# Sixteen copies of the bias table in DRAM, and tail products from the main bias tiles

## The chip, the cores and the metric

The kernel runs on one core of one Trainium2 chip. A time is device microseconds of one execution. TensorE is called PE here, VectorE DVE, ScalarE ACT, GpSimd POOL and SyncE SP, as in the profile. The core has 16 DMA engines, which serve all its queues: SP and ACT issue hardware DMAs (queues q1 and q10 of the profile), POOL issues software DMAs (q0), which can also convert from float32 to bfloat16 on the way.

## What is computed

Attention with a relative position bias for 8 batches, 8 heads, 576 positions and 64 dimensions each, and behind it a bilinear feed-forward layer:

```python
scores = scale * np.matmul(q, k.transpose(0, 1, 3, 2))      # scale = 1/8
bias = bias_table[bucket]                                   # bucket: of |i - j|, 32 buckets, table 32 x 8
scores = scores + bias.transpose(2, 0, 1)[None, :, :, :]
attn = softmax(scores)                                      # over the last axis
x = (attn @ v), heads side by side                          # 4608 x 512
out = ((x @ w_a) * (x @ w_b)) @ w_out                       # w_a, w_b: 512 x 1536, w_out: 1536 x 512
```

All inputs and the output are float32. Distances of 128 and more have one bucket, the last. The softmax does not change if that bucket's bias is taken from every score, so a product with exp(bias - last bias) is needed only near the diagonal.

## The kernel before

**Tiling.** Heads are worked in 32 pairs: pair p is batch p // 4 and heads 2 (p % 4) and the next. The 576 positions are 4 tiles of 128 (the main part) and a tail of 64. For a pair, `qk1(p, t)` computes the transposed scores of key tile t against 512 queries for both heads, `ex(p, t)` (L346, ACT) takes exp, `mul(p, t)` (L354, DVE) multiplies the blocks near the diagonal with the bias tile `W_sb[p % 4]`. `qk_tail` and `ex_tail` (L373, L374) do the same for scores with tail keys or tail queries, into `att_sb`. `mul_tail(p)` (L380, L383) multiplies the tail's blocks near the diagonal: columns 896 to 1088 of `att` (tail keys against the last query tile and the tail queries), and a block of the last key tile against the tail queries. In these columns the partitions 0 to 63 belong to the first head of the pair and 64 to 127 to the second. `av` (L396, L405) multiplies with v, whose extra column of ones gives the sum, and `norm` (L413, L414) divides.

**The bias.** bt_sb is the table less its last row (L207, DVE), eb_sb its exp (L218, ACT). A product with a one-hot matrix (L220, PE) gives exp(bias) by distance, 256 entries for each head, copied into tab_sb between ones (L223, DVE) and written to a DRAM tensor `bias_tab` of 8 x 512 bfloat16 (L224, SP). From it the bias tiles are read back with a shift of one element per partition: `W_sb[hp]` (L167), 128 partitions x 2 heads x 384 elements, so 256 packets of 768 B; and `Wt_sb` (L228), a table for the tail, 64 partitions x 4 pairs x 192 elements for each of two heads, so 512 packets of 384 B in two DMAs. All partitions of one W read from the same two rows of 1 KB.

**The start.** For batch 0, q and k of pairs 0 to 2 come as float32 over SP and ACT (L130, `load32`), with their tails (L146, `load_pad`), and are transposed on PE (L511, L552). `warm_up` (L214) is matmuls on zeros. POOL clears buffers until 9.35 us, and then issues, in this order: v of batch 0, its tail, q and k of pair 3, w_a and w_b in parts (L159), q and k of batch 1, v of batch 1, more of w_a and w_b, q and k of batch 2 and their tails, w_out as one DMA (L164, tile `wo`), v of batch 2 and so on. `gate(2)` and `gate(3)` hold the loads of W2 and W3 on SP until DVE has come to a point of pairs 0 and 1.

**The order of the work.** It is written out by hand: the code's order is each engine's order (`manual_schedule`). The first four pairs run in a loop of their own, L561 and following lines; from pair 4 on each step weaves units of the feed-forward layer (`ff_a` L460 and L464, `ff_b` L470 and L473, `ff_o` L480 and L484) between the parts of attention. The units run in the order of 512-row chunks, so the first `ff_o` of chunk 0 comes in the step of pair 8; it is the first to need `wo`. From pair 8 on q and k are transposed by DMA instead of PE (`turn`, L322 and L327, SP), and the attention output of most pairs also (`t_x`, L429 and L432, SP). Every DMA carries one of 8 semaphores of its kind (8 for hardware DMAs, 8 for software DMAs), in turn, and is issued only when the eighth before it has landed.

Of the kernel before, what the change touches and what calls it, by code (L numbers as in the profile page):

```python
# [13 lines left out]
def kernel(  # L14
# [11 lines left out]
    nc = tc.nc  # L26
    FP32 = mybir.dt.float32
    BF16 = mybir.dt.bfloat16
    ACTF = mybir.ActivationFunctionType
    MULT = mybir.AluOpType.mult  # L30

    B, H, S, Dh = 8, 8, 576, 64
    NB = 32
# [12 lines left out]
    const = ctx.enter_context(tc.tile_pool(name="const", bufs=1))  # L46
    wpool = ctx.enter_context(tc.tile_pool(name="wpool", bufs=1))
# [13 lines left out]

    NR = 256
    TB = 512
    n_arr = np.abs(np.arange(NR) - NR // 2)
    half = NB // 2
    is_small = n_arr < half
# [12 lines left out]
    cst = const.tile([128, 128 + NR], BF16, name="cst_sb")  # L79
    ident = cst[:, 0:128]  # L80
    bt_sb = const.tile([128, H], FP32, name="bt_sb")
    bl_sb = const.tile([128, H], FP32, name="bl_sb")
    eb_sb = const.tile([128, H], BF16, name="eb_sb")
    tab_sb = const.tile([128, TB], BF16, name="tab_sb")
    zero_sb = const.tile([128, 512], BF16, name="zero_sb")
    tab = nc.dram_tensor("bias_tab", [H, TB], BF16, kind="Internal")
    W_sb = [wpool.tile([128, 2, 384], BF16, name=f"W{hp}") for hp in range(H // 2)]
    Wt_sb = wpool.tile([128, H // 2, 192], BF16, name="Wt")
    att_sb = [wpool.tile([128, 1152], BF16, name=f"att{i}") for i in range(2)]
    id32 = const.tile([128, 128], FP32, name="id32")  # L90
    q32 = const.tile([128, 3, NM, 2, Dh], FP32, name="q32")
# [2 lines left out]
    kt32 = const.tile([128, H // 2, 2, Dh], FP32, name="kt32")  # L94
# [49 lines left out]
    def load_pad(eng, src, dst, b, nb):  # L144
        for hh in range(2):
            eng.dma_start(  # L146
                out=dst[64 * hh:64 * hh + 64, 4 * (b % 2):4 * (b % 2) + 4 * nb, hh, 0:Dh],
                in_=src[b:b + nb, hh:H:2, SM:S, :].rearrange("b h c d -> c (b h) d"))
# [15 lines left out]
        nc.gpsimd.dma_start(out=wo_sb[:, :, :], in_=moe_w_out.rearrange("(t p) n -> p t n", p=128))  # L164

    def load_w(eng, hp):
        eng.dma_start(out=W_sb[hp][:, :, :],  # L167
                      in_=bass.AP(tensor=tab, offset=2 * hp * TB, ap=[[1, 128], [TB, 2], [1, 384]]))

    nc.sync.dma_start(out=bt_sb[0:NB, :], in_=bias_table)  # L170
    nc.scalar.dma_start(out=cst[:, :], in_=cst_handle.ap())
# [1 line left out]
                        in_=bass.AP(tensor=bias_table.tensor, offset=(NB - 1) * H,  # L173
                                    ap=[[0, NB], [1, H]]))
    def pad(eng, x, n):
        eng.memset(x[0:64, :, 1, 0:n], 0.0)
        eng.memset(x[64:128, :, 0, 0:n], 0.0)
# [5 lines left out]
    def load32(p, src, out, engs):  # L183
        for h in range(2):
            load_h(engs[h], src, out[:, p, :, h, :], 0, 2 * p + h)
# [6 lines left out]
    nc.vector.memset(zero_sb[:, :], 0.0)  # L192
    pad(nc.vector, kt32, Dh)
    pad(nc.vector, qt32, Dh)
    load_pad(nc.scalar, k, kt32, 0, 1)
    load_pad(nc.sync, q, qt32, 0, 1)
    nc.vector.memset(tab_sb[0:H, 0:127], 1.0)
    nc.vector.memset(tab_sb[0:H, 127 + NR:TB], 1.0)
    nc.vector.tensor_copy(out=id32[:, :], in_=ident)
    for i in range(2):  # L200
        nc.vector.memset(vm[i][:, :, :, Dh:Dh + 1], 1.0)
# [3 lines left out]
        for x in (ktl, qtl):  # L205
            pad(nc.gpsimd, x[i], Dh)
    nc.vector.tensor_tensor(out=bt_sb[0:NB, :], in0=bt_sb[0:NB, :], in1=bl_sb[0:NB, :],  # L207
                            op=mybir.AluOpType.subtract)
# [3 lines left out]
    def warm_up(n):  # L212
        for _ in range(n):
            nc.tensor.matmul(out=warm[:, :], lhsT=zero_sb[:, 0:128], rhs=zero_sb[:, :],  # L214
                             start=True, stop=True)

    warm_up(7)
    nc.scalar.activation(out=eb_sb[0:NB, :], in_=bt_sb[0:NB, :], func=ACTF.Exp)  # L218
    tps = ps_av.tile([128, 512], FP32, tag="av", name="tab_ps")
    nc.tensor.matmul(out=tps[0:H, 0:NR], lhsT=eb_sb[0:NB, :], rhs=cst[0:NB, 128:128 + NR],  # L220
                     start=True, stop=True)
    warm_up(2)
    nc.vector.tensor_copy(out=tab_sb[0:H, 127:127 + NR], in_=tps[0:H, 0:NR])  # L223
    nc.sync.dma_start(out=tab.ap(), in_=tab_sb[0:H, :])  # L224
    load32(2, q, q32, (nc.sync, nc.sync))
    load_w(nc.sync, 0)
    for hh in range(2):
        nc.sync.dma_start(out=Wt_sb[64 * hh:64 * hh + 64, :, :],  # L228
                          in_=bass.AP(tensor=tab, offset=hh * TB + 192,
                                      ap=[[1, 64], [2 * TB, H // 2], [1, 192]]))  # L230
    load32(2, k, k32, (nc.sync, nc.sync))
    load_w(nc.sync, 1)

    load_v(0)
# [142 lines left out]
    def mul_tail(p):  # L377
        hp = p % 4
        at, w = att_sb[p % 2], W_sb[hp]
        nc.vector.tensor_tensor(out=at[:, 896:1088], in0=at[:, 896:1088],  # L380
                                in1=Wt_sb[:, hp, ::-1], op=MULT)
        x = at[:, 0:512].rearrange("p (h t c) -> p h t c", h=2, t=NM)[:, :, NM - 1, :]
        nc.vector.tensor_tensor(out=x, in0=x, in1=w[:, :, 127:63:-1], op=MULT)  # L383

# [172 lines left out]
    def gate(hp):  # L557
        nc.vector.memset(W_sb[hp][0:1, 0, 0:1], 0.0)
        load_w(nc.sync, hp)

    for s in range(4):  # L561
        ex(s, 0)
        if s > 0:
            mul(s - 1, 3)
            mul_tail(s - 1)
# [58 lines left out]
    for s in range(4, NP + 1):  # L624
# [37 lines left out]
        for x in steps:  # L662
            if x is U:
                seen += 1
                n = (quota * seen + nu - 1) // nu - put
# [45 lines left out]
```

The softmax here doesn't subtract the row's maximum and nothing guards it: scores larger than these inputs give would overflow.

## Time and profile before

| | us |
|---|---|
| median of 5 runs | 445.08 |
| lowest, highest | 443.13, 447.65 |
| profiled execution | 446.2 |
| its span | 444.4 |
| PE busy | 414.8 (93%) |
| ACT busy | 242.5 (55%) |
| DVE busy | 192.8 (43%) |
| POOL busy | 115.1 (26%) |
| DMA queue q0 (POOL), share of 16 engines | 66.8% |
| DMA queue q1 (SP), share of 16 engines | 33.6% |

The profile is of one execution. A busy engine is one with an instruction in flight. A group's row names the line, the engine, the operation, output <- inputs, shapes and count, then total busy time and the mean time of one in ns, then the idle time of that engine just before such instructions and what ended it. A row of the timeline has start, duration, engine, line and operation, and in brackets the idle time before it and its releaser; SPq is the issuing of a DMA on SP. In a table by stretch, each engine has its busy time and number of instructions (PE, weight loads, DVE, ACT, POOL), and then come the granted PE clock, the mean number of packets in flight on a DMA engine (DMA share, which can exceed 1), and GB/s. The trace also records each DMA packet with queue, size and duration.

### The profile page before, as it was taken

What the parts mean: (1) busy time and instruction counts of PE and PEld (TensorE: products, weight loads), DVE (VectorE), ACT (ScalarE), POOL (GpSimd) and SP (SyncE); (2) the same over time, 40 slices, a digit from 0 to 9 for tenths busy, and PEclk for the clock granted to TensorE, in tenths of its full rate; (3) what the DMA queues carried; (4) which work ended last, traced back from release to release, by engine and by line L of the source; (5) the groups of instructions that cost most, each with busy time, mean ns of one, the idle gap of its engine ahead of it and who ended that gap; (6) DMA issues with size and microseconds to landing.
All of it is one profiled execution on the core that took longest, in us unless ns stands there. A gap on an engine that the chain in (4) does not pass through costs nothing.

```text
span 444.4 us, 8320 instructions
## 1 busy us (share of the span) xinstructions
PE 414.8 (93%) x3326; PEld 204.2 (46%) x3326; DVE 192.8 (43%) x468; ACT 242.5 (55%) x344; POOL 115.1 (26%) x152
## 2 busy tenths in 40 slices
PE   7396899599999999999999999999999999999995
PEld 3164344255444444444444444444444454444442
DVE  4265465324554355525552554355535550331320
ACT  4374766356665666666665666566656642322321
POOL 8678775057313600371026101100000000000000
PEclk9779999889999999999999999999999999999999
DMA  8999999999993997299819980941021002002004
GB/s 152 154 141 132 184 164 94 170 138 180 154 147 30 122 179 96 17 147 173 98 10 131 181 100 7 169 95 38 13 86 38 15 14 97 0 1 94 0 1 94
DMA packets 177191, 42.87 MB, mean 96 GB/s; under 512 B 163704, under 2 KB 172544, under 8 KB 177152
## 3 DMA queue, kind: packets, MB, share of 16 engines
q0 software_dynamic: 113232, 17.97, 66.8%
q1 hardware_dynamic: 62176, 23.88, 33.6%
q10 hardware_dynamic: 1744, 0.49, 0.6%
q8 instruction: 26, 0.43, 0.4%
q14 instruction: 13, 0.11, 0.1%
HBM read 38.83 MB, written 9.45 MB: 109 GB/s over the span
## 4 chain that ended last, share of the span: by engine, by line
PE 79%; DMA 15%; POOL 4%; issue 1%; ACT 0%; POOLq 0%
PE po L480 22%; PE pb L470 20%; PE pa L460 19%; PE av L405 7%; PE qk L335 6%; DMA wb<-in_moe_w_b_dram 6%; DMA wo<-in_moe_w_out_dram 5%; DMA vm<-in_v_dram 2%; DMA kn<-in_k_dram 2%; PE av L396 2%; PE qkt L360 1%; PE qkt L363 1%; POOL kn L124 1%; POOL vm L124 1%; PE qktt L366 0%
## 5 line engine op out<-in xcount | busy, mean ns | idle before, releaser
L346 ACT ACTIVATE at<-qk 128x1024 bf16<-128x1024 f32 x128 | 125.8, 1024 | 22.0 <-PE qk L335 22.0
L473 DVE TENSOR_TENSOR g<-pb,ha 128x512 bf16<-128x512 f32 x108 | 74.7, 692 | 127.4 <-PE pb L470 105.2
L460 PE MATMUL pa<-xn,wa 128*128 128x512 bf16 x432 | 111.1, 379 | 0.0
L470 PE MATMUL pb<-xn,wb 128*128 128x512 bf16 x432 | 110.9, 379 | 0.0
L480 PE MATMUL po<-wo,g 128*128 128x512 bf16 x432 | 104.4, 385 | 5.4 <-DMA wo<-in_moe_w_out_dram 5.4
L464 ACT ACTIVATE ha<-pa 128x512 f32<-128x512 f32 x108 | 64.6, 598 | 77.0 <-PE pa L460 77.0
L354 DVE TENSOR_TENSOR at<-at,W 128x512 bf16<-128x512 bf16 (+1 forms) x128 | 60.2, 484 | 13.6 <-ACT at L346 10.0
L480 PEld LDWEIGHTS <-g 128*128 128x128 bf16 x432 | 38.9, 99 | 53.2 <-issue 9.7
L470 PEld LDWEIGHTS <-wb 128*128 128x128 bf16 x432 | 38.7, 97 | 53.3 <-issue 18.0
L460 PEld LDWEIGHTS <-wa 128*128 128x128 bf16 x432 | 38.8, 98 | 49.6 <-issue 10.1
L484 ACT ACTIVATE ob<-po 128x512 f32<-128x512 f32 x36 | 21.5, 597 | 69.8 <-PE po L480 69.8
L124 POOL DMA_DIRECT2D vm<-in_v_dram x32 | 28.2, 895 | 102.2 <-PE av L405 98.7
L405 PE MATMUL av<-vm,at 128*128 128x65 bf16 x1024 | 48.0, 196 | 0.0
L405 PEld LDWEIGHTS <-at 128*128 128x128 bf16 x1024 | 43.3, 99 | 6.6
L413 DVE RECIPROCAL rc<-av 128x6 f32<-128x6 f32 x64 | 12.1, 189 | 59.6 <-PE av L405 59.6
L396 PE MATMUL av<-vt,att 128*128 128x130 bf16 x160 | 35.4, 221 | 0.4 <-DMA vt<-in_v_dram 0.4
L414 DVE TENSOR_TENSOR XG<-av,rc 128x384 bf16<-128x384 f32 x64 | 31.4, 491 | 4.2 <-DMA xn<-XG 2.1
L374 ACT ACTIVATE att<-qkt 128x1024 bf16<-128x1024 f32 x32 | 32.7, 1022 | 0.0
L124 POOL DMA_DIRECT2D qn<-in_q_dram x28 | 24.8, 906 | 25.5 <-DMA wo<-in_moe_w_out_dram 13.0
L335 PE MATMUL qk<-QTb,KTb 64*128 64x512 bf16 x192 | 29.1, 381 | 0.0
L124 POOL DMA_DIRECT2D kn<-in_k_dram x28 | 24.7, 892 | 14.1 <-DMA vt<-in_v_dram 6.6
L396 PEld LDWEIGHTS <-att 128*128 128x128 bf16 x160 | 15.9, 99 | 8.2 <-issue 0.9
(99 smaller groups left out, 204.8 us busy)
## 6 DMA issues: line engine op xcount, KB each, us to landing
out_dram<-ob SPq DMA_DIRECT2D x32, 256.0 KB, 3.7
vm<-in_v_dram POOLq DMA_DIRECT2D x32, 128.0 KB, 7.1
qn<-in_q_dram POOLq DMA_DIRECT2D x28, 128.0 KB, 10.8
kn<-in_k_dram POOLq DMA_DIRECT2D x28, 128.0 KB, 14.5
wa<-in_moe_w_a_dram POOLq DMA_DIRECT2D x6, 256.0 KB, 7.2
wb<-in_moe_w_b_dram POOLq DMA_DIRECT2D x6, 256.0 KB, 8.6
wo<-in_moe_w_out_dram POOLq DMA_DIRECT2D x1, 1536.0 KB, 22.3
out_dram<-ob SPq DMA_DIRECT2D x8, 128.0 KB, 2.3
```

Source lines behind the costliest of these rows:

```text
L124: nc.gpsimd.dma_start(out=(vm[b % 2][:, h0:h1, t, 0:Dh] if dst is None else dst[b % 2][:, :].rearrange("p (t h d) -> p t h d", h=H, t=NM)[ ...
L335: nc.tensor.matmul(out=ps[:, hh, :], lhsT=kT_(p, t)[r, :], rhs=qT[r, :, :], start=True, stop=True)
L346: nc.scalar.activation(out=at[:, :, :], in_=ps[:, :, :], func=ACTF.Exp, scale=scale)
L354: nc.vector.tensor_tensor(out=at[:, :, lo:hi], in0=at[:, :, lo:hi], in1=w[:, :, y:(None if z < 0 else z):-1], op=MULT)
L374: nc.scalar.activation(out=at[:, 0:1024].rearrange("p (a x) -> p a x", a=2), in_=ps[:, :, :], func=ACTF.Exp, scale=scale)
L396: nc.tensor.matmul(out=pav[:, slot, :, :], lhsT=x, rhs=vt[b // 2 % 2][:, 4 * i + hp, :, :], start=True, stop=True)
L405: nc.tensor.matmul(out=pav[:, slot, hh, :], lhsT=x, rhs=vm[i][:, 2 * hp + hh, t, :], start=False, stop=True, skip_group_check=True)
L460: nc.tensor.matmul(out=pa[:, :], lhsT=wa_sb[df // FW][:, mc, 128 * (df % FW):128 * (df % FW) + 128], rhs=xn_sb[mc][:, xin(c)], start=(mc = ...
L464: nc.scalar.activation(out=ha[:, :], in_=pa[:, :], func=ACTF.Copy)
L470: nc.tensor.matmul(out=pb[:, :], lhsT=wb_sb[df // FW][:, mc, 128 * (df % FW):128 * (df % FW) + 128], rhs=xn_sb[mc][:, xin(c)], start=(mc = ...
L473: nc.vector.tensor_tensor(out=g_sb[df][:, :], in0=pb[:, :], in1=ff["ha"][:, :], op=MULT)
L480: nc.tensor.matmul(out=po[:, :], lhsT=g_sb[df][:, 128 * tt:128 * tt + 128], rhs=wo_sb[:, df, :], start=(df == 0), stop=(df == NDF - 1))
```

## The change

- The DRAM table holds 16 copies of the 8 rows, 128 rows in all. To make them, exp is taken with a broadcast input into 16 x 8 columns of eb_sb, the one-hot product has 128 output rows, and the copy, the cleared borders and the write to DRAM have 128 rows.
- `load_w` becomes two DMAs, one for each head, of 128 packets of 768 B. Partitions 8r to 8r + 7 read from copy r.
- The tail table `Wt_sb` and its two DMAs are gone. `mul_tail` multiplies the 64 partitions of each head with the matching slice of `W_sb`, so it has three DVE instructions instead of two.
- On ACT, the load of the tails of k for batch 0 is issued behind exp instead of ahead of the bias memsets in the code's order.
- One warm-up matmul instead of two behind the one-hot product.

```diff
--- before.py
+++ after.py
@@ -61,6 +61,7 @@
 
     NR = 256
     TB = 512
+    NREP = 128 // H
     n_arr = np.abs(np.arange(NR) - NR // 2)
     half = NB // 2
     is_small = n_arr < half
@@ -80,12 +81,11 @@
     ident = cst[:, 0:128]
     bt_sb = const.tile([128, H], FP32, name="bt_sb")
     bl_sb = const.tile([128, H], FP32, name="bl_sb")
-    eb_sb = const.tile([128, H], BF16, name="eb_sb")
+    eb_sb = const.tile([128, NREP * H], BF16, name="eb_sb")
     tab_sb = const.tile([128, TB], BF16, name="tab_sb")
     zero_sb = const.tile([128, 512], BF16, name="zero_sb")
-    tab = nc.dram_tensor("bias_tab", [H, TB], BF16, kind="Internal")
+    tab = nc.dram_tensor("bias_tab", [NREP * H, TB], BF16, kind="Internal")
     W_sb = [wpool.tile([128, 2, 384], BF16, name=f"W{hp}") for hp in range(H // 2)]
-    Wt_sb = wpool.tile([128, H // 2, 192], BF16, name="Wt")
     att_sb = [wpool.tile([128, 1152], BF16, name=f"att{i}") for i in range(2)]
     id32 = const.tile([128, 128], FP32, name="id32")
     q32 = const.tile([128, 3, NM, 2, Dh], FP32, name="q32")
@@ -164,8 +164,11 @@
         nc.gpsimd.dma_start(out=wo_sb[:, :, :], in_=moe_w_out.rearrange("(t p) n -> p t n", p=128))
 
     def load_w(eng, hp):
-        eng.dma_start(out=W_sb[hp][:, :, :],
-                      in_=bass.AP(tensor=tab, offset=2 * hp * TB, ap=[[1, 128], [TB, 2], [1, 384]]))
+        for hh in range(2):
+            eng.dma_start(
+                out=W_sb[hp][:, hh, :],
+                in_=bass.AP(tensor=tab, offset=(2 * hp + hh) * TB,
+                            ap=[[H * TB + 128 // NREP, NREP], [1, 128 // NREP], [1, 384]]))
 
     nc.sync.dma_start(out=bt_sb[0:NB, :], in_=bias_table)
     nc.scalar.dma_start(out=cst[:, :], in_=cst_handle.ap())
@@ -192,10 +195,9 @@
     nc.vector.memset(zero_sb[:, :], 0.0)
     pad(nc.vector, kt32, Dh)
     pad(nc.vector, qt32, Dh)
-    load_pad(nc.scalar, k, kt32, 0, 1)
     load_pad(nc.sync, q, qt32, 0, 1)
-    nc.vector.memset(tab_sb[0:H, 0:127], 1.0)
-    nc.vector.memset(tab_sb[0:H, 127 + NR:TB], 1.0)
+    nc.vector.memset(tab_sb[:, 0:127], 1.0)
+    nc.vector.memset(tab_sb[:, 127 + NR:TB], 1.0)
     nc.vector.tensor_copy(out=id32[:, :], in_=ident)
     for i in range(2):
         nc.vector.memset(vm[i][:, :, :, Dh:Dh + 1], 1.0)
@@ -215,19 +217,17 @@
                              start=True, stop=True)
 
     warm_up(7)
-    nc.scalar.activation(out=eb_sb[0:NB, :], in_=bt_sb[0:NB, :], func=ACTF.Exp)
+    nc.scalar.activation(out=eb_sb[0:NB, :].rearrange("n (r h) -> n r h", h=H),
+                         in_=bt_sb[0:NB, :].unsqueeze(1).to_broadcast([NB, NREP, H]), func=ACTF.Exp)
+    load_pad(nc.scalar, k, kt32, 0, 1)
     tps = ps_av.tile([128, 512], FP32, tag="av", name="tab_ps")
-    nc.tensor.matmul(out=tps[0:H, 0:NR], lhsT=eb_sb[0:NB, :], rhs=cst[0:NB, 128:128 + NR],
+    nc.tensor.matmul(out=tps[:, 0:NR], lhsT=eb_sb[0:NB, :], rhs=cst[0:NB, 128:128 + NR],
                      start=True, stop=True)
-    warm_up(2)
-    nc.vector.tensor_copy(out=tab_sb[0:H, 127:127 + NR], in_=tps[0:H, 0:NR])
-    nc.sync.dma_start(out=tab.ap(), in_=tab_sb[0:H, :])
+    warm_up(1)
+    nc.vector.tensor_copy(out=tab_sb[:, 127:127 + NR], in_=tps[:, 0:NR])
+    nc.sync.dma_start(out=tab.ap(), in_=tab_sb[:, :])
     load32(2, q, q32, (nc.sync, nc.sync))
     load_w(nc.sync, 0)
-    for hh in range(2):
-        nc.sync.dma_start(out=Wt_sb[64 * hh:64 * hh + 64, :, :],
-                          in_=bass.AP(tensor=tab, offset=hh * TB + 192,
-                                      ap=[[1, 64], [2 * TB, H // 2], [1, 192]]))
     load32(2, k, k32, (nc.sync, nc.sync))
     load_w(nc.sync, 1)
 
@@ -377,8 +377,10 @@
     def mul_tail(p):
         hp = p % 4
         at, w = att_sb[p % 2], W_sb[hp]
-        nc.vector.tensor_tensor(out=at[:, 896:1088], in0=at[:, 896:1088],
-                                in1=Wt_sb[:, hp, ::-1], op=MULT)
+        for hh in range(2):
+            r, y = slice(64 * hh, 64 * hh + 64), 383 - 64 * hh
+            nc.vector.tensor_tensor(out=at[r, 896:1088], in0=at[r, 896:1088],
+                                    in1=w[r, hh, y:y - 192:-1], op=MULT)
         x = at[:, 0:512].rearrange("p (h t c) -> p h t c", h=2, t=NM)[:, :, NM - 1, :]
         nc.vector.tensor_tensor(out=x, in0=x, in1=w[:, :, 127:63:-1], op=MULT)
 
```

## The prediction

> **What bounds the kernel now.** I read the page first: span, engine shares, costliest groups.
>
> ```profile
> span 444.4 us, 8320 instructions
> ...
> PE 414.8 (93%) x3326; PEld 204.2 (46%) x3326; DVE 192.8 (43%) x468; ACT 242.5 (55%) x344; POOL 115.1 (26%) x152
> ...
> L480 PE MATMUL po<-wo,g 128*128 128x512 bf16 x432 | 104.4, 385 | 5.4 <-DMA wo<-in_moe_w_out_dram 5.4
> ```
>
> PE is idle for 444.4 − 414.8 = 29.6 us. A table of busy time by stretch shows where:
>
> ```profile
> 10.00:15.00 5.00, 3.12 (x23) 1.63 (x21) 1.40 (x3) 4.29 (x7) 5.00 (x8) 1.00 1.09 114
> 15.00:20.00 5.00, 0.00 (x0) 0.00 (x0) 2.70 (x8) 0.94 (x2) 2.12 (x3) 0.76 2.04 156
> ...
> 70.00:80.00 10.00, 9.31 (x80) 4.69 (x81) 5.73 (x15) 6.49 (x9) 3.52 (x5) 1.00 1.44 106
> 80.00:90.00 10.00, 4.57 (x36) 2.24 (x35) 3.05 (x8) 2.54 (x3) 0.88 (x1) 0.79 1.41 166
> 90.00:100.00 10.00, 10.00 (x86) 4.89 (x85) 3.11 (x9) 5.65 (x8) 5.24 (x6) 0.86 2.08 136
> 100.00:444.00 344.00, 339.52 (x2610) 162.73 (x2608) 145.33 (x337) 188.62 (x271) 53.84 (x65) 1.00 0.79 82
> ```
>
> The first number after the stretch is its length, the second PE's busy time; the last three are clock, DMA share, GB/s. From 100 to 444 PE lacks 4.48 us, all at the end, after its last matmul. So nothing there is worth time unless it stops PE, and the whole question is what happens before 88 us. Two waits stand there, in the timeline:
>
> ```profile
> 11.67 1.43 SPq L130 DMA_DIRECT2D k<-in_k_dram  x2
> 15.27 0.91 DVE L354 TENSOR_TENSOR at<-at,W 128x512 bf16<-128x512 bf16 x2 [3.65 <-DMA W<-bias_tab]
> 21.09 1.09 PE L511 MATMUL trk<-id,k 128*128 128x128 f32 x4 [6.54 <-DMA k<-in_k_dram]
> ...
> 65.39 1.02 POOL L164 DMA_DIRECT2D wo<-in_moe_w_out_dram  x1 [0.49 <-DMA kn<-in_k_dram]
> ...
> 87.75 1.89 PE L480 MATMUL po<-wo,g 128*128 128x512 bf16 x4 [5.43 <-DMA wo<-in_moe_w_out_dram]
> ```
>
> The second one decides. At 82.3 PE has nothing left that does not need wo and stands until 87.75. Whatever PE gains or loses before that, up to 5.43 us, disappears in this wait; only the landing of wo moves the end. Wo is late in POOL's queue, whose DMAs each wait for the eighth one before (this shows as waits for other loads):
>
> ```profile
> 16.18 0.75 POOL L130 DMA_DIRECT2D kn<-in_k_dram  x1 [0.55 <-DMA vm<-in_v_dram]
> 18.46 0.74 POOL L130 DMA_DIRECT2D kn<-in_k_dram  x1 [1.53 <-DMA vm<-in_v_dram]
> 20.32 0.74 POOL L159 DMA_DIRECT2D wa<-in_moe_w_a_dram  x1 [1.11 <-DMA vm<-in_v_dram]
> 23.00 0.74 POOL L159 DMA_DIRECT2D wb<-in_moe_w_b_dram  x1 [1.94 <-DMA vm<-in_v_dram]
> ```
>
> From 15.6 us on POOL issues as fast as its earlier loads land. So the change is worth what it gives to POOL's queue between its first load (9.35, first packets at 11.25) and about 30 us, when the bias tables have been read.
>
> **What the Trainium skill says.** (1) "DMA: Bandwidth & Descriptors", Queues, rings and completion order: each DMA engine takes turns between the queues that have work, packet by packet. The trace agrees: while W is read (12 to 13 us) POOL's queue moves 249 packets of 128 B, at 17 to 18 us, beside other loads of SP, 609. (2) The same page, Latency and other measured facts, has DMA rates halved by row pitches of 2 MiB and more and supposes aliased memory channels; on many engines reading one small table it says nothing. Here the same 768-B packets took 74 ns on average for W0, 51, 65 and 40 for W1 to W3, and 42 for the load of cst (128 different rows). (3) "VectorE: DVE Perf Modes", Two Vector instructions with no wait between them: an instruction that starts in another group of 32 partitions than the one before is held until that has finished. The trace has no such pair; it shows what is lost, L380 and L383 starting 0.17 us apart although L380 lasts 0.25. (4) "TensorE: Matmul & The Clock Gate", Part 1: an idle window of about 3.4 us halves the clock. The trace agrees: after the wait for wo it is 0.5 from 86.13 to 92.96, which costs PE half of 92.96 − 87.75, or 2.6 us.
>
> **The change, part by part, as time of POOL's queue.** The yardstick is the rate of all queues together where W isn't read: 863, 839 and 900 packets a us at 14, 15 and 17 us, so about 860.
>
> - Wt goes: 2 DMAs of 256 packets, 512 / 860 = 0.60 us, and 1.26 us of SP's issuing.
> - W0 from 16 copies: from 11.47 to 14.0 the engines moved 1,171 packets in 2.53 us, where 860 a us would be 2,176. The gap is 1,005 / 860 = 1.17 us. POOL's supply doesn't explain it (0.88 us for each 1,024 packets). But the copies only spread the reads over 16 places, 8,208 B apart, and each place still has 8 readers. Bounds 0 (no cure) and 1.2; I take 0.9.
> - W1 to W3: (11 + 25) ns × 256 above W3's 40 ns, over 16 engines, is 0.58 us; with a DMA share of some 1.6 (that many packets at once) it is 0.35. Bounds 0 and 0.6.
> - The order on SP. Hardware DMAs too wait for the eighth before them, and the moved kt load and the added W DMA shift these pairs: the k loads of pair 1 waited until 4.77 for a q load, and now wait for cst and the bias table, landed by 3.7. Exp waits only for the subtraction at 4.61 (0.36 us earlier, as the table load no longer stands behind the kt issues). Against it the table write grows from 8 to 128 packets, at 79 ns 8 on each engine instead of one, so 0.55 us more before W0. What of W0 is read before 11.25 meets no load of POOL. Bounds 0 and 1.0; I take 0.2.
>
> Sum 0.60 + 0.9 + 0.35 + 0.2 = 2.05 us; bounds 0.6 and 3.4.
>
> Costed at nothing:
> - The k load of pair 2 stands behind W0 alone instead of W0 and Wt. It should land near 17 instead of 21, PE restart, and then wait for vm and vt (23.5 now, earlier by about the sum). That is PE's gain, and it vanishes in the wait for wo. W's wait at 15.27 likewise.
> - The kt DMAs now stand on ACT behind exp, before the copy of QT (6.44): exp ends near 4.9, two issues take 1.35, so 6.25; they wait for a q and a k load that land near 5. They land 4.8 us after issue, near 10.4, for a transpose at 10.17. A slip of 1 us here reaches PE, but PE stands from 14.55 to 21.09 behind it. Four more SP issues of about 0.37 us for W, against two of Wt: SP waits for DVE's gates at 13 to 23 anyway.
> - The first W multiply waits for two DMAs instead of one; the second comes 0.4 us behind. Behind it on DVE is the copy of QT for pair 1 (18.91), which PE needs only after the k load.
> - Exp over 128 instead of 8 elements: at most the 0.38 us of the 256-wide copy instead of 0.21. The table product has 128 rows instead of 8 at the same 256 columns. One warm-up matmul (0.3 us) less, inside PE's wait for k and q.
> - The tail product: two of 0.25 us instead of one, held: 0.25 + 0.25 + 0.22 against 0.39 from L380's start to L383's end, +0.33 us, 32 times, 10.6 us of DVE (lower bound 0.17 each, if they overlap). Cover: I took every tail product from 100 to 366 us. The next DVE instruction starts at least 0.88 us after it, and the matmul that reads att at least 0.61 us after (once; else 1.25 or more). Without that cover it would be 28 × 0.33 = 9.2 us.
>
> The profiled execution took 446.2 us (span 444.4 and 1.8 around it), so 446.2 − 2.05 = 444.15. It lies 1.1 above the median of the runs, 445.08; against the median that is 443.0.
>
> **Rivals.**
> - The clock. If wo lands 2 us earlier and PE arrives at its wait no earlier, the wait is 3.4 us, and the half clock behind it (2.6 us) may be spared. 443.0 − 2.6 = 440.4. For: the wait would be as short as one window. Against: PE's start is freed too, and arrives earlier by about as much.
> - The reads are not cured: slow because of their odd byte offsets, or because 8 KB apart is the same place again. For: the offsets stay. Against: W3, with the same offsets, took 40 ns when it ran thinly. Only Wt's 0.6 us remains: 444.4.
> - Slower: the DMA transposes fall deeper into wo. Wo took 22.3 us because SP's transposes of qn, kn and XG run in it: 49 and 53 GB/s in 72 to 76 against 179 and 196 in 78 to 82. One us of that costs 1 − 51/185 = 0.72 us. They are issued in order, when PE, DVE and the qn and kn loads allow, and the change brings all of these forward by different amounts. From 2.05 / 0.72 = 2.8 us more overlap on, the kernel is slower than before. One more stretch of 4 us with the gain eaten gives 445.1 + 2.9 = 448.0; two, 450.9. Against: what they wait for are mostly POOL's own loads, which move with wo.
>
> **How the numbers follow.** Forecast 443.0 (441.7 to 444.2) has 0.50, the clock 0.18 (439 to 441.5), no cure 0.18 (444 to 445.5), slower 0.14 (446 to 451). The range 439.3 to 447.8 leaves out the ends of the clock case and the upper half of the slow case. A difference of 1% (4.45 us) is about what a measurement of this kernel can tell from no change. Faster by that, below 440.6: most of the clock case and the far tail of the forecast, 0.23. Slower, above 449.5: 0.09. Between: 0.68.
>
> **What would show it.** W's packets at 40 to 50 ns each; no wait for Wt; the k load of pair 2 landed near 17 us; POOL's kn, wa and wb issues 1 to 2 us earlier; the wait for wo ending near 85.7 instead of 87.75; DVE busy some 5 to 10 us more with PE still full from 100 us on. The prediction is wrong if wo's landing doesn't follow POOL's early issues (then the transposes decide), or if PE shows gaps behind tail products.

## The result, and the profile after

The changed kernel takes 444.23 us (median of 44 runs, 441.75 to 446.77); the kernel before, in runs beside it, 444.13 us (79 runs). The ratio is 1.0011, with a 95% interval of 0.9997 to 1.0024: no gain, and at most a quarter of a per cent of loss. Ratios here and below leave out executions that are over 1.5% above the fastest of their kernel and are estimated apart from the medians, which are of all executions, so they are not quite the quotients of these. The forecast was 443.0, range 439.3 to 447.8, with 0.68 for "within 1%". The range held, and so did "within 1%"; the 2.05 us of gain did not come, so the question is where they went.

The page of the changed kernel's profiled execution (445.21 us, of which 443.4 are its span), with the groups and the landing of `wo` that answer to those read before:

```profile
span 443.4 us, 8351 instructions
...
PE 415.0 (94%) x3325; PEld 204.7 (46%) x3325; DVE 203.4 (46%) x500; ACT 242.7 (55%) x344; POOL 115.1 (26%) x152
...
L482 PE MATMUL po<-wo,g 128*128 128x512 bf16 x432 | 103.2, 382 | 0.0
...
L335 PE MATMUL qk<-QTb,KTb 64*128 64x512 bf16 x192 | 29.5, 386 | 4.0 <-DMA KTb<-kn 4.0
...
L382 DVE TENSOR_TENSOR att<-att,W 64x192 bf16<-64x192 bf16 x64 | 15.9, 249 | 11.5 <-ACT att L374 11.0
...
wo<-in_moe_w_out_dram POOLq DMA_DIRECT2D x1, 1536.0 KB, 15.0
```

The wait of 5.4 us for `wo` is gone. In its place PE waits 4.0 us for `KTb`, the transposed k that SP's queue delivers. DVE has 10.6 us more work (203.4 against 192.8), nearly all of it in the tail product. Before, its first part was one instruction for each pair, 8.0 us in all (shortest, median and longest in ns):

```profile
L380 DVE TENSOR_TENSOR att<-att,Wt x32: 246/248/260, 18.6 to 360.7; 128x192 bf16<-128x192 bf16 x32
```

Now it is two, L382, 15.9 us in all; the rest of the 10.6 us is that the products of a tail no longer overlap. The table by stretch says where PE stands (length, then PE's busy time first; clock, DMA share and GB/s last):

```profile
10.00:15.00 5.00, 3.58 (x27) 2.07 (x26) 2.08 (x4) 4.57 (x7) 5.00 (x8) 1.00 0.96 91
15.00:20.00 5.00, 0.54 (x4) 0.10 (x2) 2.44 (x9) 1.93 (x3) 2.12 (x3) 0.92 1.87 167
...
70.00:80.00 10.00, 8.89 (x73) 4.33 (x72) 6.27 (x15) 5.84 (x10) 1.55 (x2) 1.00 1.35 168
80.00:90.00 10.00, 7.09 (x77) 3.86 (x74) 5.07 (x13) 5.29 (x8) 3.04 (x5) 1.00 1.97 132
90.00:100.00 10.00, 8.91 (x80) 4.61 (x81) 3.06 (x8) 4.85 (x7) 5.67 (x7) 0.83 1.99 163
100.00:444.00 344.00, 338.68 (x2605) 162.26 (x2603) 153.09 (x361) 187.85 (x269) 50.57 (x61) 1.00 0.76 79
```

From 100 us to the end of the span (343.4 us) PE lacks 4.7 us, much as the 4.48 us before (up to 444 us): the added DVE work costs nothing there. Everything is again decided before 92 us, in the timeline:

```profile
10.55 1.22 SPq L168 DMA_DIRECT2D W<-bias_tab  x2
11.81 1.14 SPq L130 DMA_DIRECT2D k<-in_k_dram  x2
...
17.51 0.91 DVE L354 TENSOR_TENSOR at<-at,W 128x512 bf16<-128x512 bf16 x2 [4.90 <-DMA W<-bias_tab]
18.50 0.75 POOL L130 DMA_DIRECT2D kn<-in_k_dram  x1 [2.13 <-DMA vm<-in_v_dram]
20.28 0.74 POOL L159 DMA_DIRECT2D wa<-in_moe_w_a_dram  x1 [1.03 <-DMA vm<-in_v_dram]
22.25 1.08 PE L513 MATMUL trk<-id,k 128*128 128x128 f32 x4 [6.71 <-DMA k<-in_k_dram]
22.61 0.74 POOL L159 DMA_DIRECT2D wb<-in_moe_w_b_dram  x1 [1.58 <-DMA vm<-in_v_dram]
...
63.40 1.02 POOL L164 DMA_DIRECT2D wo<-in_moe_w_out_dram  x1 [0.22 <-issue]
...
91.09 1.03 PE L335 MATMUL qk<-QTb,KTb 64*128 64x512 bf16 x4 [4.00 <-DMA KTb<-kn]
```

Almost nothing of the start has moved as forecast. The k of pair 2 is issued at 11.81 us, later than the 11.67 of before although the two loads of Wt between W0 and it are gone, and PE gets it at 22.25 instead of 21.09. The first product with W starts at 17.51 instead of 15.27. POOL's `kn`, `wa` and `wb` stand within 0.4 us of where they were (18.46, 20.32, 23.00). The issue of W0 takes 1.22 us (two DMAs) where one took 0.37 before:

```profile
9.95 0.37 SPq L167 DMA_DIRECT2D W<-bias_tab  x1
```

One caution: single executions of one kernel differ by 2 to 3 us in this stretch, as the runs below show. Times are therefore compared over many runs; a trace is only one execution, and counts for more where several kernels with the same edit agree.

### The profile page after: what moved, and what is told of

Same layout as the page of the kernel before. It is cut to its first block, busy times and chain, and to the rows that moved or that the text cites. A ratio compares the mean times of both kernels' runs of the same rounds, so it can differ in the third digit from the quotient of the medians.

```text
span 443.4 us, 8351 instructions
## 1 busy us (share of the span) xinstructions
PE 415.0 (94%) x3325; PEld 204.7 (46%) x3325; DVE 203.4 (46%) x500; ACT 242.7 (55%) x344; POOL 115.1 (26%) x152
## 4 chain that ended last, share of the span: by engine, by line
PE 85%; DMA 9%; DVE 2%; SPq 1%; ACT 1%; issue 1%; DVEq 0%; ACTq 0%
PE pb L472 22%; PE po L482 21%; PE pa L462 21%; PE av L407 8%; PE qk L335 7%; DMA KTb<-kn 3%; DMA k<-in_k_dram 2%; DMA xn<-XG 2%; PE av L398 2%; PE qkt L360 1%; PE qkt L363 1%; DMA q<-in_q_dram 1%; DMA bias_tab<-tab_sb 1%; ACT at L346 1%; DVE g L475 0%
## 5 line engine op out<-in xcount | busy, mean ns | idle before, releaser
L482 PE MATMUL po<-wo,g 128*128 128x512 bf16 x432 | 103.2, 382 | 0.0
L382 DVE TENSOR_TENSOR att<-att,W 64x192 bf16<-64x192 bf16 x64 | 15.9, 249 | 11.5 <-ACT att L374 11.0
```

The costliest lines, as they stand in the source:

```text
L482: nc.tensor.matmul(out=po[:, :], lhsT=g_sb[df][:, 128 * tt:128 * tt + 128], rhs=wo_sb[:, df, :], start=(df == 0), stop=(df == NDF - 1))
```

## The experiments

Times are medians, each ratio is against runs of the kernel before on the same chip. Where an expectation names a theory by a letter, the text around it says in words what is told apart.

### One part at a time

First: does the gain never arise, or does one part of the change give it and another take it? Four kernels, made from the kernel before. `p1_copies` has the 16 copies and the W loads in two DMAs, and keeps `Wt`:

```diff
+    NREP = 128 // H
...
+    tab = nc.dram_tensor("bias_tab", [NREP * H, TB], BF16, kind="Internal")
...
+        for hh in range(2):
+            eng.dma_start(
+                out=W_sb[hp][:, hh, :],
+                in_=bass.AP(tensor=tab, offset=(2 * hp + hh) * TB,
+                            ap=[[H * TB + 128 // NREP, NREP], [1, 128 // NREP], [1, 384]]))
```

> The kernel before with only the 16 copies and the W loads in two DMAs; tail table, order on ACT and warm-ups stay. Theory A (two chains of nearly equal length end at about 88 to 91 us: POOL's queue up to w_out, and table write, W0, k of pair 2, PE, XG, DMA transpose of k of batch 2; the larger table write makes the second longer): W0's multiply and the k of pair 2 come 0.5 to 1.5 us later than in before, ratio 1.001 to 1.004. Rival B (the start hardly matters, reads from copies cost the same as before): ratio 0.999 to 1.001, no shift. If the copies do cure the reads (the prediction): W packets at 40 to 50 ns, ratio 0.996 to 0.998.

Measured: 444.7 us, ratio 1.0013 [0.9993, 1.0033]. The copies alone give nothing; a loss of up to 0.3% is not excluded.

`p2_tail` has the tail product from W, and no `Wt`, with the table as before:

```diff
-    for hh in range(2):
-        nc.sync.dma_start(out=Wt_sb[64 * hh:64 * hh + 64, :, :], ...)
...
+        for hh in range(2):
+            r, y = slice(64 * hh, 64 * hh + 64), 383 - 64 * hh
+            nc.vector.tensor_tensor(out=at[r, 896:1088], in0=at[r, 896:1088],
+                                    in1=w[r, hh, y:y - 192:-1], op=MULT)
```

> The kernel before with only the tail product from the main W tiles (no tail table, three DVE instructions in a tail product); one table of 8 rows. Theory A: 512 packets less on both chains, k of pair 2 lands 1 to 2 us earlier, ratio 0.995 to 0.998. Rival B: ratio 0.999 to 1.001. A third reason, the longer tail product reaching PE: 1.005 or more, with gaps of PE behind tail products after 100 us.

Measured: 442.48 us, ratio 0.9943 [0.9921, 0.9966], so 2.5 us faster (1.5 to 3.5 by the interval; the medians differ by 1.95). Its timeline:

```profile
10.00 0.37 SPq L166 DMA_DIRECT2D W<-bias_tab  x1
10.41 1.03 SPq L129 DMA_DIRECT2D k<-in_k_dram  x2
14.69 0.91 DVE L349 TENSOR_TENSOR at<-at,W 128x512 bf16<-128x512 bf16 x2 [1.90 <-DMA W<-bias_tab]
17.64 1.09 PE L508 MATMUL trk<-id,k 128*128 128x128 f32 x4 [1.91 <-DMA k<-in_k_dram]
...
21.63 0.27 PE L393 MATMUL av<-vt,att 128*128 128x130 bf16 x1 [1.74 <-DMA vt<-in_v_dram]
...
86.05 1.89 PE L477 MATMUL po<-wo,g 128*128 128x512 bf16 x4 [5.57 <-DMA wo<-in_moe_w_out_dram]
```

With Wt out of the way k is issued 1.3 us earlier than before, PE has it 3.4 us earlier (17.64 against 21.09), and the first product with v starts at 21.63 instead of 23.70. The wait for `wo` is as long as before, but ends 1.7 us earlier (86.05 against 87.75).

`p3_order` moves the kt loads on ACT behind exp and drops the warm-up matmul:

```diff
-    load_pad(nc.scalar, k, kt32, 0, 1)
...
     nc.scalar.activation(out=eb_sb[0:NB, :], in_=bt_sb[0:NB, :], func=ACTF.Exp)
+    load_pad(nc.scalar, k, kt32, 0, 1)
...
-    warm_up(2)
+    warm_up(1)
```

> The kernel before with only the load of the tails of k moved behind exp on ACT and one warm-up matmul less. Theory A: the copy of QT on ACT and the first scores come up to 1 us later, but the table is written earlier; ratio 0.999 to 1.002. Rival B: 0.999 to 1.001. Were the later tails of k what eats the gain: 1.003 or more, with PE waiting for kt.

Measured: 444.89 us, ratio 0.9993 [0.9973, 1.0014]: harmless and useless. Its single trace has `wo` issued at 62.53 instead of 65.39 us, with no gain in the runs: an earlier issue of `wo` in one trace, as in the changed kernel's, is no proof of one.

`p0_notable` takes the bias tables away, to see what all their traffic costs. The table is neither written nor read, and every bias weight is one:

```diff
-    nc.sync.dma_start(out=tab.ap(), in_=tab_sb[0:H, :])
...
-    load_w(nc.sync, 0)
-    for hh in range(2):
-        nc.sync.dma_start(out=Wt_sb[64 * hh:64 * hh + 64, :, :], ...)
...
+    nc.vector.memset(W_one[:, :, :], 1.0)
```

> The kernel before with no bias table in DRAM at all: the write and all reads of W and Wt are left out, and the products near the diagonal are with ones, so the bias is left out of the scores. The most that any cheaper reading of the table could give. Theory A: the k of pair 2 lands near 13 instead of 21 us, then PE waits for v of batch 0 at about 21 to 22; both chains get about 2 us shorter; ratio 0.993 to 0.996. Rival B (the start hardly matters): 0.998 to 1.001. If the prediction's yardstick for the reads is right (all reads together cost POOL's queue some 3 us): 0.992 to 0.995 and the issue of w_out 3 us earlier.

Measured: 438.17 us, ratio 0.9851 [0.9818, 0.9883]. The bias traffic and SP's order around it cost 6.6 us, more than any of its expectations allowed. The k of pair 2 is there without a wait, and the first product with v starts 5.5 us earlier than before:

```profile
15.90 0.66 PE L501 MATMUL trk<-id,k 128*128 128x128 f32 x4
...
18.17 0.22 PE L386 MATMUL av<-vt,att 128*128 128x130 bf16 x1 [0.92 <-DMA vt<-in_v_dram]
```

The three parts alone multiply to 1.0013 × 0.9943 × 0.9993 = 0.9949; the whole has 1.0011, further off than their intervals together allow. They interact.

### Which part takes the gain

The tail part was put together with each of the other two. `p12_copies_tail` is the changed kernel without the edits of `p3_order`:

```diff
+    tab = nc.dram_tensor("bias_tab", [NREP * H, TB], BF16, kind="Internal")
...
-    Wt_sb = wpool.tile([128, H // 2, 192], BF16, name="Wt")
```

> The kernel before with the copies and with the tail product from W, but the old order on ACT and two warm-up matmuls. The tail part alone gave 0.9943, because the k of pair 2 landed at 17.6 instead of 21.1 us. Theory C: the copies take this back, since W0 in two DMAs is issued in 1.2 instead of 0.4 us, starts later and is no faster: k of pair 2 at 20 to 22.5 us, ratio 0.998 to 1.002. Rival D (the order on ACT takes it back): k of pair 2 at 17 to 18.5, ratio 0.993 to 0.996.

Measured: 444.67 us, ratio 1.0002 [0.9987, 1.0017].

`p23_tail_order` is the changed kernel without the copies:

```diff
-    load_pad(nc.scalar, k, kt32, 0, 1)
...
+    load_pad(nc.scalar, k, kt32, 0, 1)
...
-    Wt_sb = wpool.tile([128, H // 2, 192], BF16, name="Wt")
```

> The kernel before with the tail product from W and the new order on ACT, without the copies. Theory C: k of pair 2 at 17 to 18.5 us, ratio 0.993 to 0.996. Rival D: k of pair 2 at 20 to 22.5, ratio 0.998 to 1.002.

Measured: 442.52 us, ratio 0.9947 [0.9928, 0.9967]. So the moved loads on ACT leave the gain of the tail part alone, and the copies, which cost nothing clear by themselves, take all of it. Why they cost less beside `Wt` was not found. In the timeline of the kernel with copies and tail part:

```profile
9.93 1.21 SPq L168 DMA_DIRECT2D W<-bias_tab  x2
11.18 1.14 SPq L130 DMA_DIRECT2D k<-in_k_dram  x2
16.39 0.91 DVE L354 TENSOR_TENSOR at<-at,W 128x512 bf16<-128x512 bf16 x2 [3.59 <-DMA W<-bias_tab]
19.87 1.08 PE L513 MATMUL trk<-id,k 128*128 128x128 f32 x4 [4.14 <-DMA k<-in_k_dram]
```

W0 is asked for at the same time as in `p2_tail` (9.93 and 10.00), but it is issued for 1.21 us instead of 0.37, DVE has it 1.7 us later, and k 2.2 us later. These two executions took 444.34 us (`p2_tail`) and 441.97 (`p12_copies_tail`), the other way round from the medians: they show where the start differs, not that the difference in time comes from there. The records of W0's packets (768 B each, 256 of them; times from the timeline's zero) over the kernels that read it in this place, `d_pe_a` and `d_pool_a` of below included:

| kernel | copies | first packet after issue, us | first packet to last end, us | mean ns of a packet |
|---|---|---|---|---|
| before | no | 1.3 | 3.3 | 74 |
| p2_tail | no | 1.3 | 3.0 | 74 |
| p23_tail_order | no | 1.0 | 3.0 | 60 |
| p3_order | no | 1.4 | 2.4 | 50 |
| after | yes | 2.2 | 4.3 | 63 |
| p12_copies_tail | yes | 2.0 | 4.0 | 86 |
| p1_copies | yes | 1.9 | 3.2 | 69 |
| d_pe_a | yes | 1.8 | 3.7 | 72 |
| d_pool_a | yes | 1.4 | 2.6 | 65 |

With copies the packets are no faster, and in four of the five kernels they start 0.4 to 1.1 us later after the issue than without. The fifth, `d_pool_a`, starts as early as `p3_order`: there POOL's first packets move only at 15.3 us instead of 11.0. So it seems to take both for the late start, the longer issue and POOL's loads, which set in just as W0's packets are due; `d_pool_a` is a single trace.

### Is it the shared rows, and do 16 copies cure them?

`m_styles` reads 128 rows of 768 B from the table in a quiet stretch (375 to 432 us), two reads of each pattern one after the other, in three rounds:

```diff
+    styles = {"hot": [[1, 128], [1, 384]], "hot0": [[0, 128], [1, 384]],
+              "cop": [[H * TB + 8, 16], [1, 8], [1, 384]],
+              "own": [[TB + 1, 128], [1, 384]], "own0": [[TB, 128], [1, 384]]}
```

> The changed kernel, and near its end, where the DMA engines do little, 30 reads of 128 rows of 768 B from the table, pairs of reads one after the other, in five patterns three times: all partitions from one row with a shift of an element each (as before); all from one row without a shift; 16 copies as in the change; each partition its own row with a shift; each its own row without one. Only the packets count, not the time of the kernel. If many readers of one row are what is slow: the first two 70 ns, the others 36 to 45. If the odd start is: with a shift 49 or more, without 36, copies or not. If neither, and only other traffic makes them slow: all near 40.

Measured (one execution, whose total time says nothing here). The first read of each pattern overlaps the last of the pattern before it, so the table has the second reads, three of each, from the packet records and SP's issues:

| pattern | mean ns of a packet | first packet to last end, us | issue to last end, us |
|---|---|---|---|
| one row for all, shifted by an element per partition (W of before) | 61 to 71 | 1.62 to 1.67 | 2.6 to 2.75 |
| one row for all, not shifted | 39 to 54 | 1.50 to 1.59 | 2.45 to 2.55 |
| 16 copies, 8 shifted readers each (W of the changed kernel) | 52 to 60 | 1.19 to 1.21 | 2.5 |
| a row for each partition, shifted | 41 to 50 | 0.52 to 0.60 | 1.5 to 1.55 |
| a row for each partition, not shifted | 36 to 49 | 0.56 to 0.84 | 1.5 to 1.8 |

The landings over all reads (KB, median us from issue to landing):

```profile
scr_hot<-bias_tab SPq DMA_DIRECT2D x12, 96.0 KB, 3.5
scr_own<-bias_tab SPq DMA_DIRECT2D x12, 96.0 KB, 1.9
...
scr_cop<-bias_tab SPq DMA_DIRECT2D x6, 96.0 KB, 3.6
```

The names `hot` and `own` cover both forms, with and without shift. The odd start is not what is slow: a row of its own with the shift is as quick as without. A read in which many readers share one place is slow: 1.6 us against 0.55. With 8 readers in each of 16 places the packets are through in 1.2 us, so the copies spare 0.4 of the 1.1 us that rows of their own would. And most of that is given back in the issue: SP takes 0.52 us for the second read of the copies, 0.32 for the second reads of the other patterns, and the first packet follows 1.3 instead of 1.0 us after the issue. From issue to end the copies are nearly as slow as the single row, 2.5 against 2.6 to 2.75 us.

The single packet is not what grows. Its median is 34 to 44 ns in every pattern; what differs is how many are under way at once, on average 3 to 4 for the unshifted single row, 5 for the shifted one, 6 for the copies, 7 to 11 for rows of their own. The expectation, which looked at the time of a packet, does not decide here. Whether DRAM or the handing out of the packets to the engines holds them back was not tested.

### Is it the order on SP?

If the copies do harm because k of pair 2 stands behind a W0 that takes longer, putting k ahead of W0 must give the gain back. `a1_k_first` does that to the changed kernel, and `v1_k_first` to `p2_tail`:

```diff
     load32(2, q, q32, (nc.sync, nc.sync))
-    load_w(nc.sync, 0)
     load32(2, k, k32, (nc.sync, nc.sync))
+    load_w(nc.sync, 0)
     load_w(nc.sync, 1)
```

> The tail part alone, and the two loads of the k of pair 2 issued ahead of W0 on SP, in the time in which SP waits for the table write. Theory C (SP's chain over this k decides what PE has done when the transposes and w_out come): k lands by 15 us, PE next waits for v of batch 0 at 20 to 22 us, ratio 0.989 to 0.993. Rival E (only POOL's queue up to w_out sets the end): no better than the tail part alone, 0.993 to 0.996.

> The changed kernel with only the two loads of the k of pair 2 issued ahead of W0 on SP. Theory C (the copies take the gain of the tail part back because this k waits behind W0 and its longer issue): k lands by 16 us, the gain is back, ratio to before 0.992 to 0.996. Rival F (what the copies cost is the later W0 itself, and with it the first products on DVE): W0 even later, ratio 0.998 to 1.002.

Measured: `v1_k_first` 441.49 us, 0.9928 [0.9904, 0.9952]; `a1_k_first` 442.53 us, 0.9968 [0.9949, 0.9988]. The first interval holds values of both its theories. The second ratio is just above what its theory C expected (0.992 to 0.996); against the changed kernel's 1.0011 it is 0.43%, or 1.9 us, better. First the timeline of `v1_k_first`, then that of `a1_k_first`:

```profile
9.11 1.05 SPq L129 DMA_DIRECT2D k<-in_k_dram  x2
14.42 0.91 DVE L349 TENSOR_TENSOR at<-at,W 128x512 bf16<-128x512 bf16 x2 [1.83 <-DMA W<-bias_tab]
15.45 0.66 PE L508 MATMUL trk<-id,k 128*128 128x128 f32 x4
```

```profile
8.70 0.92 SPq L130 DMA_DIRECT2D k<-in_k_dram  x2
10.41 11.34 SPq L168 DMA_DIRECT2D W<-bias_tab  x8
15.46 0.66 PE L513 MATMUL trk<-id,k 128*128 128x128 f32 x4
16.61 0.90 DVE L354 TENSOR_TENSOR at<-at,W 128x512 bf16<-128x512 bf16 x2 [4.02 <-DMA W<-bias_tab]
20.82 0.74 POOL L159 DMA_DIRECT2D wb<-in_moe_w_b_dram  x1 [0.96 <-DMA vm<-in_v_dram]
21.06 0.27 PE L398 MATMUL av<-vt,att 128*128 128x130 bf16 x1 [4.24 <-DMA vt<-in_v_dram]
```

In `a1_k_first` the k is issued 3.1 us earlier than in the changed kernel. By the packet records it is read by 12 us, while POOL's first packets move from 11.1 us on; in the changed kernel it is read from 15 to 21 us, among POOL's. POOL's `wb` follows 1.8 us earlier than in the changed kernel. So one moved line brings 1.9 us back, and that k stands behind W0 costs time in the changed kernel. How much of the copies' harm this is remains open. The same line may help without copies too: from `p2_tail` to `v1_k_first` the ratio falls by 0.15%, with some 0.3% of uncertainty. And with k ahead of W0 the copies still cost 0.4% (0.9968 against 0.9928, uncertain by 0.3%), where with W0 ahead they cost 0.6% (1.0002 against 0.9943, and 1.0011 against 0.9947, also uncertain by 0.3% or a little less). In the two kernels with k first, k reaches PE at the same time (15.46 and 15.45), but the first product with W starts 2.2 us later with copies. That is rival F of the expectation, the later W0 itself: it was not separated from the added issues.

### PE's start, or the DMA queues?

The k arrives earlier at PE, but do these 1.9 us come from PE? Two kernels delay one thing in the changed kernel. `d_pe_a` repeats the four transposes of k for pair 3 eleven times:

```diff
-        for t in range(NM):
+        for t in list(range(NM)) * (11 if p == 3 else 1):
```

> The changed kernel with the bf16 transposes of k of pair 3 done 11 times over (the result is the same), some 3 us of PE at about 29 us. Theory G (in the changed kernel PE's start sets when the transposes are issued, and PE ends up waiting for that of k of batch 2): 1.5 to 3 us later, ratio 1.003 to 1.007. The prediction's reading (PE's start is covered by the wait for w_out, only POOL's queue counts): 0.999 to 1.002.

Measured: 444.29 us, 0.9986 [0.9959, 1.0013]. From its timeline:

```profile
19.42 1.09 PE L513 MATMUL trk<-id,k 128*128 128x128 f32 x4 [3.69 <-DMA k<-in_k_dram]
...
28.03 2.63 PE L307 MATMUL trk<-cst_sb,kn 128*128 128x128 bf16 x44
...
90.06 0.60 PE L335 MATMUL qk<-QTb,KTb 64*128 64x512 bf16 x4 [1.45 <-DMA KTb<-kn]
```

PE works 2.2 us more at 28 us (2.63 instead of 0.40), and the kernel is no slower. The wait for `KTb` is 1.45 us where the changed kernel's trace has 4.00. A delay of PE at this point is covered. (The first line shows the spread of single executions: up to 28 us this is the changed kernel, and its k came at 19.42 instead of 22.25.)

`d_pool_a` holds back POOL's first load by six memsets:

```diff
+    for _ in range(3):
+        pad(nc.gpsimd, qtl[1], Dh)
     load_v(0)
```

> The changed kernel with six more memsets of 0.52 us on POOL ahead of its first load, so its whole queue is 3.3 us later. The prediction's reading (only POOL's queue counts): 3 us later, ratio 1.006 to 1.008. Theory G alone, with 5 us of slack between the landing of w_out and its use: 0.999 to 1.003; as v of batch 0 and k of batch 2 are POOL's loads too, and PE and the transposes wait for them, some of it may show: up to 1.005.

Measured: 446.48 us, 1.0041 [1.0018, 1.0065]; against the changed kernel 0.30% (uncertain by 0.27%), or 1.3 us, for 3.47 us of delay, and less than the prediction's reading asked for.

```profile
12.82 3.54 POOL L124 DMA_DIRECT2D vm<-in_v_dram  x4
14.30 0.91 DVE L356 TENSOR_TENSOR at<-at,W 128x512 bf16<-128x512 bf16 x2 [1.75 <-DMA W<-bias_tab]
15.41 0.66 PE L515 MATMUL trk<-id,k 128*128 128x128 f32 x4
...
24.39 0.27 PE L400 MATMUL av<-vt,att 128*128 128x130 bf16 x1 [7.63 <-DMA vt<-in_v_dram]
```

A delay of POOL's queue reaches the end, if barely clear of the noise, but part of it is paid back: its first packet moves at 15.3 us, and before that W0 lands undisturbed (last end at 13.8 us, in the changed kernel 17.0) and k is read (from 12 to 15 us instead of 15 to 21). That fits the prediction's reading that both queues live off the same DMA engines: what counts is what they have moved together by some 22 us. That the gain of k first comes by this way is argued from these traces, not isolated.

If so, starting POOL's loads earlier must help. `v2_v_early` has the tail part, k first, and POOL's clearing of the second buffers behind its loads of v:

```diff
+    def clear(i):
         pad(nc.gpsimd, vt[i], Dh + 1)
...
+        if i == 0:
+            clear(i)
...
     load_vt(0, 1)
+    clear(1)
```

> The tail part, k of pair 2 ahead of W0, and POOL's memsets for the second buffers (4 us) moved behind the loads of v of batch 0, so that these start at about 5.5 instead of 9.3 us. PE waited 3.9 us for this v in the version with k first alone. If v is next: PE's wait for it gone, w_out issued 2 to 3 us earlier, ratio 0.985 to 0.990. If the loads of v only push W0 and k of pair 2 back by as much: 0.991 to 0.996.

Measured: 439.48 us, 0.9897 [0.9855, 0.994], the best of all, with POOL's loads 3.7 us and `wb` 5.3 us earlier than before:

```profile
5.62 3.54 POOL L123 DMA_DIRECT2D vm<-in_v_dram  x4
...
17.75 0.79 POOL L158 DMA_DIRECT2D wb<-in_moe_w_b_dram  x1
```

It was run with other kernels than `v1_k_first`, and the two intervals overlap: that moving POOL's clearing adds to k first is not shown.

### All kernels side by side

The start of the first product with v needs v's landing, and everything ahead of it on PE, k of pair 2 among it. It sorts the kernels nearly by their times:

| kernel | first product with v starts at, us | ratio |
|---|---|---|
| p0_notable | 18.17 | 0.9851 |
| v2_v_early | 19.89 | 0.9897 |
| v1_k_first | 20.67 | 0.9928 |
| a1_k_first | 21.06 | 0.9968 |
| p2_tail | 21.63 | 0.9943 |
| p23_tail_order | 21.67 | 0.9947 |
| d_pe_a | 22.23 | 0.9986 |
| p12_copies_tail | 22.61 | 1.0002 |
| p3_order | 22.93 | 0.9993 |
| before | 23.70 | 1 |
| after | 24.29 | 1.0011 |
| p1_copies | 24.29 | 1.0013 |
| d_pool_a | 24.39 | 1.0041 |

It is a mark of how far the two queues have come, not itself the cause: a PE delay just behind it cost nothing in `d_pe_a`. The late waits are no such mark. PE waits for `wo` in before, p2_tail and p23_tail_order (5.1 to 5.6 us) and for `KTb` in after, p1_copies, p3_order and d_pool_a (3.4 to 4.3 us), and kernels with equal times stand on both sides. Which of the two is late goes with how long after the issue of `wo` PE comes to the last transposes of q ahead of this stretch (`trq`, which wait 1.11 us for `XG`; 70.69 us in before, 72.36 in after), upon which SP issues transposes of XG. Over the 14 traces, where PE comes up to 8.4 us after the issue, `wo` lands 18.7 to 23.2 us after it; where PE comes 9.0 us or more after it, 14.4 to 15.4 us, and PE then waits for `KTb` alone. This sorts single executions; it was not tested.

The granted clock is a part of the differences that was not separated either. It falls to a half in stretches of 3.4, 6.8 or 10.2 us. Up to 100 us the trace of before has 17.1 us of it (17.63 to 27.87 and 85.90 to 92.72), that of after 13.7, that of `p0_notable` 3.4. If half of PE's busy time in these stretches is lost, that is an estimated 5.7, 5.1 and 1.7 us, so up to 4 of the 6.6 us of `p0_notable` may be clock.

## Why the prediction was right and wrong, step by step

In short: the change has two halves that cancel. The tail part is worth 2.5 us, and the copies take it back. Part of what they take goes through the load of k that stands behind them on SP; how large a part, and what the rest is, stayed open.

- **"Wt goes: 2 DMAs of 256 packets, 512 / 860 = 0.60 us"**: direction right, size off. The term measured 2.5 us (0.9943). It counted the packets and left the 1.26 us of SP's issuing out of the sum. But Wt stood ahead of k of pair 2, and with it gone k's packets moved from 16 to 21 us to 13 to 17 us, out of POOL's way by as much. That this is what exceeds the 0.60 is argued, not measured by itself.
- **"W0 from 16 copies" (0.9 us) and "W1 to W3" (0.35 us)**: failed, the value was at the lower bound, 0, or below it. In the quiet, 8 readers per place save 0.4 us of 1.6 for 128 rows and lose most of it in the issue (`m_styles`). In the start W0's packets took 63 ns against 74, but over 4.3 us instead of 3.3. The term priced the time of a packet, which is not what the shared rows change. The prediction named this case (8 readers in each place, "not cured") and gave it 0.18.
- **"The order on SP" (0.2 us)**: not measured by itself, probably of the wrong sign. The table write is issued 0.6 us earlier with the moved kt loads, as it hoped (6.64 us, 7.26 before), but lands later, and W0 is not asked for earlier (10.55, 9.95 before). The 0.55 us for the larger write did not show: with the old order on ACT 128 KB landed in 2.5 us (`p1_copies`, `p12_copies_tail`). The added W DMA was taken as issues of "about 0.37 us for W", under SP's waits for DVE. An issue of the three-level pattern takes 0.6 us in this stretch, and W0's two stand in front of k. The first packet of W0 follows 0.9 us later after its issue than before. With k ahead of W0, 1.9 us come back (`a1_k_first`).
- **"It should land near 17 instead of 21"** for k of pair 2: right for the tail part alone (17.64 and 17.45), wrong for the whole (22.25; 19.42 and 19.87 in its closest kin).
- **"Only the landing of wo moves the end"**: half right. A delay of PE at 28 us is covered, as it said (`d_pe_a`), and POOL's queue counts (`d_pool_a`). But the earlier k of pair 2, put at nothing because PE's gain "vanishes in the wait for wo", was worth 1.9 us when its load alone was moved (`a1_k_first`), by PE or by the queues. And `wo` is one of two late transfers. In the changed kernel it landed 15.0 us after its issue instead of 22.3, PE did not wait for it at all, and then stood 4.00 us for `KTb` until 91.09. The forecast end of the wait for `wo`, 85.7, has nothing to be compared with.
- **The added DVE work, 10.6 us, hidden**: right to the number. The Trainium skill, "VectorE: DVE Perf Modes", Two Vector instructions with no wait between them, says that the second is held because it starts in another group of partitions. The trace now has such pairs and agrees: two products of 249 ns on partitions 0 to 63 and 64 to 127 take 0.52 us from the first's start to the second's end (0.51 at 156 us). The prediction's "The trace has no such pair" was a misreading: before, DVE's memsets of kt and qt, 64 partitions each and in turn on the lower and the upper half, last 0.27 us and start 0.36 us apart. `p2_tail` has all of these pairs too, and is faster.
- **Costed at nothing: the kt loads on ACT, the warm-up matmul, the wider exp**: right for the first two (`p3_order` 0.9993, `p23_tail_order` as `p2_tail`); exp took 0.31 us instead of 0.21, and the kernel with it and the copies shows no clear loss (`p1_copies` 1.0013).
- **Rivals.** "The reads are not cured" came nearest: 444.4 forecast, 444.23 measured, right that the reads are not cured. Its reasons were not: a shift alone is quick on rows of their own, and 8 KB apart is not quite the same place again (1.2 us against 1.6). Its remainder was right by accident: Wt gives four times its 0.6 us, and the copies eat it. The clock's saving came in part and went elsewhere: behind the late wait the half clock lasts 3.4 us (90.84 to 94.25) instead of 6.8, but there are 3.4 us of it at 43.05 to 46.47, where the trace of before has none. The slower case, transposes deeper in `wo`, was not tried by itself; `wo` landed faster here, not slower.
- **Readings.** The prediction's times of packets and of the clock lie 0.24 us late against the timeline: POOL's first packets move at 11.0, not 11.25, and the half clock behind `wo` runs from 85.90 to 92.72, so it cost 2.5 us, not 2.6. Its 249 and 609 packets of POOL show that the queues share the engines, not that they take turns. No conclusion hangs on either. The 0.23 for "below 440.6" is more than the whole clock case with 0.18, which is only in part below it.

## What to carry to other kernels

A DMA that gives way on a queue can be worth more than its own packets: look which load moves forward behind it, and whether it then lands before the competing queue starts. Splitting a load into more DMAs, or giving its pattern one more level, holds back what stands behind it (here W0's issue, 1.22 us instead of 0.37), and can eat the gain of the part beside it. Before copying a table to spread its readers, measure the read by itself with as many readers per place as the plan leaves, its issue included; here only a row for each reader was quick.

## What the runs showed of the hardware that was not expected

- Reading 128 rows of 768 B in the quiet: 1.5 to 1.7 us when all come from one row, 1.2 us from 16 copies, 0.5 to 0.8 us from 128 rows. A start shifted by one 2-byte element per row makes no difference of that size, and the median packet takes 34 to 44 ns in all of them.
- The write of the table, 128 KB instead of 8, need not take longer. In `p1_copies` (first line) and `p12_copies_tail` it landed 2.5 us after its issue; before, W0, which waits for the 8 KB, could follow 2.69 us after the write. In the changed kernel (second line) it took 3.8 us. In all kernels with the kt loads moved on ACT it was slow, with 128 KB (3.2 to 3.8 us) as with 8 (W0 followed 3.1 to 3.8 us after in `p23_tail_order` and `p3_order`).

```profile
bias_tab<-tab_sb SPq DMA_DIRECT2D x1, 128.0 KB, 2.5
bias_tab<-tab_sb SPq DMA_DIRECT2D x1, 128.0 KB, 3.8
```

- A delay of 3.47 us in one busy queue cost 1.3 us, because the other queue's transfers, freed of it, were through 3 us (W0) and 6 us (k) earlier.
